# Gated mix of attention and mixer-MLP on one core: layer-norm passes on GpSimd, buffers given back by the last matmul of a group, and a first chunk in four PSUM banks

## The chip, the core and the metric

The kernel runs on one core of a Trainium2 chip. A core has five engines with instruction queues of their own: TensorE (PE in the profile, its weight loads PEld), VectorE (DVE), ScalarE (ACT), GpSimd (POOL) and SyncE (SP, which here only issues transfers). They meet through semaphores. The metric is the device time of one execution in microseconds (us); the time before is 756.24 us, the median of three runs (755.15 to 756.38).

## What is computed

The input x is 2048 x 512 in bf16. Two branches read it and are mixed row by row by a gate:

```python
g = sigmoid((x * gate_w).sum(-1, keepdims=True))
a = softmax(q @ k.T * 16**-0.5) @ v @ wo          # 32 heads of 16, q, k, v = x @ wqkv
h = gelu(layernorm(x) @ w1)                       # 512 x 512
x1 = x + shift(h) @ w2                            # four quarters of h moved by 1, -1, 2, -2 rows
b = x1 + gelu(layernorm(x1) @ w3) @ w4            # 512 x 1792, 1792 x 512
out = g * a + (1 - g) * b
```

## The kernel before

**Work.** The rows are four chunks of 512. A round of attention is one chunk of queries, one group of 8 heads (128 columns of q) and one parity: four heads, one per 32-row strip of TensorE. A round has 64 tiles of scores (16 key tiles by four heads), each 128 keys by 512 queries in one PSUM bank; there are 32 rounds and 2048 tiles. A score matmul is L1313, a PV matmul L1537. The exponential of a tile is taken in one of two ways:

- by ScalarE (L1408), mostly two banks at a time, into `prob`;
- by VectorE (L1439) as an affine map onto the bits of bf16, followed by three shifted copies (L1482 on VectorE, L1484 on GpSimd) of a pair of tiles; all four copies go through PV with weights V or V2, which corrects the map.

The end of a round (`finish_round`, L1548) copies the accumulator (L1558), sends the denominators through DRAM and back, multiplies on GpSimd (L1576) into `oT`, and packs `oT` into `oD` by four transfers (L1580).

**The other work** fills TensorE's time between scores. Projections and MLP matmuls are groups (`gen`, L956; matmuls L964), four column tiles wide, each with one PSUM bank and an evacuation, mostly on VectorE (k L1023, q L1046, V L1063, w1 L1179, w2 L1190, w3 L1211). The gelus run on ScalarE over whole buffers: L1181 once, L1218 four times.

**Layer norms** (`normalise`, L1128): statistics on VectorE (L1122), the reciprocal root on GpSimd (L1131, L1133), then four passes per chunk on VectorE (L1142) from `x_sb` into one of two `xn` buffers, a write to DRAM (L1146), and four transposing loads (L1152) into one of two `xnT` slots, which the groups of w1 or w3 read. There are eight such chunks, four for each norm.

**The start.** 11 matmuls on zeros (L943); 16 transposes of the first chunk's x (L996) into two banks, two quarters each; copies by ScalarE and VectorE (L1006); the q projection, masked into two parities by VectorE (L1038, L1040); the k projection, copied by ScalarE (L1019); then scores.

**The tail.** After the last PV matmul VectorE turns the denominators (L1913 to L1916) and scales (L1926), while TensorE adds in its banks the output projection of head groups LG and above (`known`) and the MLP's result (`add_y`), both at L1890; then the last round's output matmuls (L1932), two evacuations each on VectorE and ScalarE (L1937, L1935), and the output transfers.

**What sets the order.** While the program is built, a planner (`Sim`, `pe_pick`) models the engines with the costs written in the code and picks what each engine issues next; the picks are then emitted as fixed queues. Its parameters (`BASE`, and `STEPS` for every 8 tiles' stage) set priorities. Buffers (`Buf`) are counted: a buffer has `users`, and an op's `frees` are counted off when it is done; at zero the slot goes to the next user. An operation marked `port` on GpSimd is made to wait for the last such operation on VectorE that was emitted before it. In a group, the four column tiles advance separately (`Gen.take`):

```python
o = self.units[k][j]
if min(self.cp) == self.cp[j]:
    for x in self.units[k]:
        if x is not o:
            o.frees += x.frees
            x.frees = []
```

## Time and profile before

| | us |
|---|---|
| median of three runs | 756.24 |
| profiled execution | 755.0 |
| span, first to last instruction | 753.0 |
| PE busy | 738.9 |
| ACT busy | 732.4 |
| DVE busy | 685.8 |
| POOL busy | 458.2 |

The profile is of one execution. A busy PE is modelled from pipelined matmuls and is not PE at its peak. Rows of a timeline give start, duration, engine, line, operation, tiles and count, and in brackets the idle time before and what ended it. Rows of groups give busy us and mean ns of one, then idle time before. In the list of waits the three numbers are us in total, how often, and the longest.

### The profile page before, as it was taken

The numbers are of one execution on the slowest core, as the hardware profiler recorded it, in microseconds if no ns is written. First come the engines' busy times: TensorE is split into PE (matmuls) and PEld (weight loads), VectorE is DVE, ScalarE is ACT, GpSimd is POOL, SyncE is SP. The second block draws the span as 40 slices with busy tenths as digits, with TensorE's granted clock in tenths as the row PEclk, the third lists the DMA queues.
The fourth block names the chain that finished last, engine by engine and source line by source line (L and its number), as shares of the span: only waits on it lengthen the run. The fifth ranks groups of instructions, "written<-read, shape, count | busy, mean of one in ns | idle before, by whom it ended". The sixth has DMA issues, their size and how long they took to land.

```text
span 753.0 us, 23698 instructions
## 1 busy us (share of the span) xinstructions
PE 738.9 (98%) x9520; PEld 213.2 (28%) x9520; DVE 685.8 (91%) x1422; ACT 732.4 (97%) x768; POOL 458.2 (61%) x456
## 2 busy tenths in 40 slices
PE   8999999999999999998999999999999999999997
PEld 4324322223222222222322222222222223222222
DVE  5999999998999999997999999998989999887897
ACT  6999999999999999998999999999999999999995
POOL 2274686657866676665544545557657877774542
PEclk9999999999999999999999999999999999999999
DMA  9403331221123220025001100012000000101001
GB/s 199 143 4 79 68 85 33 66 66 44 57 61 73 69 55 21 21 72 114 8 24 27 38 26 24 10 30 52 21 20 18 20 6 27 28 24 28 20 7 46
DMA packets 67093, 34.59 MB, mean 46 GB/s; under 512 B 46748, under 2 KB 62380, under 8 KB 66984
## 3 DMA queue, kind: packets, MB, share of 16 engines
q1 hardware_dynamic: 66040, 32.56, 17.0%
q8 instruction: 74, 1.21, 0.7%
q10 hardware_dynamic: 944, 0.52, 0.2%
q14 instruction: 35, 0.29, 0.1%
HBM read 17.40 MB, written 6.81 MB: 32 GB/s over the span
## 4 chain that ended last, share of the span: by engine, by line
PE 85%; DVE 5%; ACT 4%; DMA 4%; issue 1%; POOL 0%; SPq 0%; DVEq 0%; POOLq 0%; ACTq 0%
PE banks L1537 30%; PE banks L1313 29%; PE banks L964 24%; ACT prob L1408 3%; DMA pk<-den 2%; DVE prob L1439 2%; DVE prob L1482 1%; DMA den<-accsb 1%; ACT hT L1218 1%; PE banks L943 0%; DVE st L1122 0%; PE banks L1890 0%; DMA zE_dram<-ot 0%; POOL prob L1484 0%; DMA xnT<-xn_dram 0%
## 5 line engine op out<-in xcount | busy, mean ns | idle before, releaser
L1408 ACT ACTIVATE prob<-banks 128x1024 bf16<-128x1024 f32 (+1 forms) x747 | 687.7, 1143 | 6.3 <-PE banks L1313 5.2
L1484 POOL TENSOR_SCALAR prob<-prob 128x1024 uint16<-128x1024 uint16 x394 | 405.7, 1048 | 255.4 <-DVE prob L1482 108.7
L1439 DVE TENSOR_SCALAR prob<-banks 128x512 uint16<-128x512 f32 x551 | 364.0, 683 | 29.6 <-PE banks L1313 25.6
L1537 PE MATMUL banks<-prob,V 128*17 128x512 bf16 (+1 forms) x3707 | 318.3, 382 | 1.3 <-POOL prob L1484 0.6
L1313 PE MATMUL banks<-q,kT 32*128 32x512 bf16 x2048 | 283.2, 385 | 2.8 <-ACT prob L1408 0.9
L1482 DVE TENSOR_SCALAR prob<-prob 128x1024 uint16<-128x1024 uint16 (+1 forms) x437 | 172.6, 440 | 5.8 <-PE banks L1537 1.7
L1313 PEld LDWEIGHTS <-kT 32*128 32x128 bf16 x2048 | 70.9, 91 | 306.5 <-ACT prob L1408 277.2
L1537 PEld LDWEIGHTS <-V 128*17 128x17 bf16 (+1 forms) x3707 | 71.4, 88 | 122.4 <-issue 102.2
L964 PE MATMUL banks<-xnT,w 128*32 128x512 bf16 x1152 | 91.1, 384 | 3.4 <-DMA xnT<-xn_dram 3.4
L964 PE MATMUL banks<-w,hT 128*32 128x512 bf16 x692 | 63.2, 383 | 0.0
L964 PEld LDWEIGHTS <-w 128*32 128x32 bf16 x1920 | 39.7, 95 | 53.3 <-issue 31.4
L1576 POOL TENSOR_TENSOR oT<-accsb,bcs 128x512 bf16<-128x512 f32 x31 | 39.5, 1275 | 21.0 <-DVE prob L1482 8.4
L964 PE MATMUL banks<-w,hB 128*32 128x512 bf16 x448 | 40.0, 382 | 0.0
L964 PE MATMUL banks<-w,w 128*32 128x256 bf16 (+1 forms) x768 | 38.7, 311 | 0.6 <-DVE V L1063 0.4
L975 PE MATMUL banks<-wo,oD 32*128 32x512 bf16 x72 | 27.7, 384 | 0.0
L1211 DVE CAST hT<-banks 128x512 bf16<-128x512 f32 x28 | 19.1, 682 | 5.2 <-PE banks L964 5.2
L1211 DVE CAST hB<-banks 128x512 bf16<-128x512 f32 x28 | 19.0, 682 | 4.6 <-PE banks L964 4.5
L1558 DVE COPY accsb<-banks 128x512 f32<-128x512 f32 x31 | 21.1, 680 | 1.8 <-PE banks L1537 1.7
L964 PE MATMUL banks<-w,wq 128*32 128x512 bf16 x256 | 21.5, 390 | 0.7 <-ACT w L1006 0.7
L964 PEld LDWEIGHTS <-hT 128*32 128x32 bf16 x692 | 15.9, 95 | 20.3 <-issue 13.7
L1122 DVE BATCH_NORM_STATS2 st<-x_sb 128x6 f32<-128x512 bf16 x32 | 21.1, 678 | 0.0
L964 PE MATMUL banks<-wo,oD 128*32 128x512 bf16 x152 | 20.1, 384 | 0.1
(94 smaller groups left out, 259.1 us busy)
## 6 DMA issues: line engine op xcount, KB each, us to landing
bcs<-rr SPq DMA_DIRECT2D x124, 64.0 KB
xn_dram<-xn SPq DMA_DIRECT2D x32, 128.0 KB
w<-in_B_w_dram SPq DMA_DIRECT2D x5, 512.0 KB
oD<-oT SPq DMA_DIRECT2D x124, 16.0 KB
w<-in_B_w_dram SPq DMA_DIRECT2D x4, 448.0 KB
out_dram<-ot SPq DMA_DIRECT2D x14, 128.0 KB
x_sb<-in_A_x_dram SPq DMA_DIRECT2D x3, 512.0 KB
w<-in_A_wqkv_dram SPq DMA_DIRECT2D x2, 256.0 KB
```

Source lines behind the costliest of these rows:

```text
L964: units.append([Op("col", j, lambda j=j, lf=lf, rf=rf, n0=n0, n1=n1, st=st, sp=sp: nc.tensor.matmul(get()[32 * j:32 * j + 32, n0:n1], lhsT ...
L975: o = Op("row", i, lambda: nc.tensor.matmul(get(), lhsT=lf(0, P)[rows], rhs=rf()[rows], start=False, stop=True, tile_position=(32 * i, 0), ...
L1122: a = dve(600, deps, lambda: nc.vector.bn_stats(out=sb.slot[:], in_=x_sb[:, t, :]), prio=6, at=at, acq=[sb])
L1211: pre.append(evac(g, PSUM_NS, lambda ps, m=m: nc.vector.tensor_copy(out=h2()[:, m, :], in_=ps[:])))
L1313: o = Op("row", i, lambda: nc.tensor.matmul(dst(), lhsT=kT[G][32 * i:32 * i + 32, kt * P:(kt + 1) * P], rhs=qbuf[G, c].slot[32 * i:32 * i ...
L1408: job = act(hold, ops, lambda: nc.scalar.activation(out=prob[:, pb.cut(), :].bitcast(BF16), in_=unit()[:, rb.cut(), :], func=ACT.Exp, scal ...
L1439: return nc.vector.tensor_scalar(out=prob[:, b0.cut() if w == 2 else b0.bufs[h0].slot, :], in0=unit()[:, rb.cut() if w == 2 else rb.bufs[0 ...
L1482: return nc.vector.tensor_scalar(out=cut(k), in0=cut(0), scalar1=float(SHIFT * k), scalar2=None, op0=ALU.add)
L1484: return nc.gpsimd.tensor_scalar(out=cut(k), in0=cut(0 if both else 2), scalar1=1.0, scalar2=float(SHIFT * (k if both else 1)), op0=ALU.mu ...
L1537: return nc.tensor.matmul(one(accs[r])[32 * i:32 * i + n, :], lhsT=lhs(n), rhs=rhs(), start=st and not edge, stop=True, tile_position=(0, ...
L1558: e = dve(PSUM_NS, round_ops[r], lambda: nc.vector.tensor_copy(out=ab.slot[:], in_=one(accs[r])), acq=[ab], prio=0, frees=[accs[r], Call(a ...
L1576: n = gp(1250, d3, lambda: nc.gpsimd.tensor_tensor(out=ob.slot[:], in0=ab.slot[:], in1=bb.slot[:], op=ALU.mult), acq=[ob], frees=[ab, bb], ...
```

## The change

It has these parts:

- `normalise` runs its four passes per chunk on GpSimd, with a modelled cost of 592 ns.
- `Gen.take` hands an op's `frees` on to a column tile of the same unit that has yet to issue, instead of gathering them at the last one.
- The first chunk's transposes use four banks, one per quarter. Its k projection is split in two halves of 256 columns (`k_first`), each copied by ScalarE; scores of the first two key tiles need only the first half. The masked q for the first parity is made half by VectorE, half by ScalarE. The second chunk's four copies are all VectorE's, and its transposes wait for the first chunk's.
- The tail: LG is 3, so the groups of head groups 0 to 2 belong to the `wo` groups; `add_y` comes first, and part of the rest is put ahead of the last PV matmuls (`early`).
- Modelled costs: transfers are longer, the first gelu is longer and the later ones shorter.
- The planner's parameters (`STEPS`) are another table; the whole plan is made anew with it. The table is cut below.

```diff
@@ -157,11 +157,10 @@
             return None
         self.cp[j] += 1
         o = self.units[k][j]
-        if min(self.cp) == self.cp[j]:
-            for x in self.units[k]:
-                if x is not o:
-                    o.frees += x.frees
-                    x.frees = []
+        rest = [i for i in range(4) if self.cp[i] < self.cp[j]]
+        if rest:
+            self.units[k][rest[-1]].frees += o.frees
+            o.frees = []
         return o
 
     def row_piece(self, free, know, least):
@@ -479,7 +478,7 @@
     FT = F // P
     assert (S, D, F) == (2048, 512, 1792)
     COL = True
-    LG = 2
+    LG = 3
 
     QAT = 91
     QDUE = 75
@@ -525,211 +524,183 @@
...
@@ -903,7 +874,7 @@
     sim.t_free["SP"] = issue["SP"]
 
     def load_xT(c, k, part, prio):
-        return dma(3100.0, [], lambda: xT_dma(c, part, k)(nc.sync), hold=1280.0, prio=prio,
+        return dma(3500.0, [], lambda: xT_dma(c, part, k)(nc.sync), hold=1280.0, prio=prio,
                    acq=[wb[f"x{c}{part}"]] if k == 0 else [])
 
     def wload(name, src, users):
@@ -990,36 +961,49 @@
     TOT = H * NT * NCH
 
 
-    def x_transposes(c, half, dep):
-        g = gen("t", -1, dep + [j_id], [], due=-9 + half + T1_DUE * c)
-        ks = (half, half + 2)
+    def x_transposes(c, ks, dep):
+        g = gen("t", -1, dep + [j_id], [], due=-9 + ks[0] + T1_DUE * c)
         g.units = [[Op("full", None, lambda k=k, t=t: nc.tensor.transpose(
-            out=one(g.buf).bitcast(BF16)[:, (k // 2) * 512 + t * P:(k // 2) * 512 + (t + 1) * P],
+            out=one(g.buf).bitcast(BF16)[:, ks.index(k) * 512 + t * P:ks.index(k) * 512 + (t + 1) * P],
             in_=x_sb[:, 4 * c + t, k * P:(k + 1) * P], identity=idb[:]), ns=54.0, name="t") for t in range(4)]
             for k in ks]
         g.ops = [o for u in g.units for o in u]
         g.skew = False
-        g.buf.users = 2
-        for k in ks:
-            def cp(k=k):
-                d, s_ = W(f"x{c}0")[:, k, :], one(g.buf).bitcast(BF16)[:, (k // 2) * 512:(k // 2 + 1) * 512]
-                return nc.vector.tensor_copy(out=d, in_=s_) if k % 2 else nc.scalar.copy(out=d, in_=s_)
-            j_xT[c, 0, k] = (dve if k % 2 else act)(340 if k % 2 else 500, g.units[k // 2], cp, prio=0, frees=[g.buf])
+        g.buf.users = len(ks)
+        for n, k in enumerate(ks):
+            on_dve = c or k % 2
+
+            def cp(k=k, n=n, on_dve=on_dve):
+                d, s_ = W(f"x{c}0")[:, k, :], one(g.buf).bitcast(BF16)[:, n * 512:(n + 1) * 512]
+                return nc.vector.tensor_copy(out=d, in_=s_) if on_dve else nc.scalar.copy(out=d, in_=s_)
+            j_xT[c, 0, k] = (dve if on_dve else act)(375 if on_dve else 535, g.units[n], cp, prio=0, frees=[g.buf])
 
 
     j_k = {}
+
+    def k_first():
+        for h in range(2):
+            g = gen("k0", -1, [j_xT[0, 0, 0], j_xT[0, 0, 1], dl_w["k0"]],
+                    [(lambda a, b, k=k: W("k")[:, k, a:b],
+                      lambda k=k, h=h: W("x00")[:, k, 256 * h:256 * h + 256], 0, 256, k == 0, k == KT - 1, 107.5)
+                     for k in range(KT)], due=-3 + h)
+            if h:
+                g.ops[-1].frees += [wb["k"], wb["x00"]]
+            j = act(275, g.units[-1], lambda g=g, h=h: nc.scalar.copy(out=kT[0][:, 256 * h:256 * h + 256],
+                                                                      in_=one(g.buf)[:, 0:256]), prio=0, frees=[g.buf])
+            if h:
+                j_k[0, 0] = j
+            else:
+                j_ka.append(j)
+
+    j_ka = []
 
     def k_proj(G, c, at):
         g = gen(f"k{G}", at, [j_xT[c, 0, k] for k in range(KT)] + [dl_w["k0" if G == 0 else "k"]],
                 [(lambda a, b, k=k: W("k")[:, k, G * P + a:G * P + b],
                   lambda k=k: W(f"x{c}0")[:, k, :]) for k in range(KT)])
         g.ops[-1].frees += [wb["k"], wb[f"x{c}0"]]
-        if G == 0 and c == 0:
-            g.due = -3
-            j_k[G, c] = act(500, g.units[-1], lambda: nc.scalar.copy(out=kT[G][:, 0:512], in_=one(g.buf)[:]), prio=0,
-                            frees=[g.buf])
-            return
-        g.due = 14 * c - 6 if G == 0 else g.due
+        g.due = 14 * c - 11 if G == 0 else g.due
         j_k[G, c] = evac(g, PSUM_NS, lambda ps: nc.vector.tensor_copy(out=kT[G][:, c * 512:(c + 1) * 512], in_=ps[:]),
                          prio=1)
 
@@ -1028,19 +1012,23 @@
 
     def q_proj(G, c, at):
         part = 1 if c else 0
-        g = gen(f"q{G}", at, [j_xT[c, part, k] for k in range(KT)] + [dl_w["q0" if G == 0 else "q"]],
+        g = gen(f"q{G}", at, [j_xT[c, part, k] for k in range(KT if c or G else 2)] + [dl_w["q0" if G == 0 else "q"]],
                 [(lambda a, b, k=k: wq[:, k, G * P + a:G * P + b],
                   lambda k=k: W(f"x{c}{part}")[:, k, :]) for k in range(KT)], due=at + QDUE - QAT if at >= 0 else -4)
         g.ops[-1].frees.append(wb[f"x{c}{part}"])
         qb = qbuf[G, c] = Buf("q", 128)
         if G == 0 and c == 0:
 
-            e1 = dve(680, g.units[-1] + [j_m3], lambda: nc.vector.tensor_scalar(
-                out=qb.slot[:, 0, :], in0=one(g.buf)[:], scalar1=mE[:], scalar2=None, op0=ALU.mult), prio=0, acq=[qb])
-            e2 = dve(680, [e1], lambda: nc.vector.tensor_scalar(
-                out=qb.slot[:, 1, :], in0=one(g.buf)[:], scalar1=mO[:], scalar2=None, op0=ALU.mult), prio=0,
+            e1 = [dve(345, g.units[-1] + [j_m3], lambda: nc.vector.tensor_scalar(
+                out=qb.slot[:, 0, 0:256], in0=one(g.buf)[:, 0:256], scalar1=mE[:], scalar2=None, op0=ALU.mult), prio=0,
+                acq=[qb])]
+            e1.append(act(330, g.units[-1] + [j_m3], lambda: nc.scalar.activation(
+                out=qb.slot[:, 0, 256:512], in_=one(g.buf)[:, 256:512], func=ACT.Copy, scale=mE[:]), prio=0))
+            e1[1].need = qb
+            e2 = dve(680, e1, lambda: nc.vector.tensor_scalar(
+                out=qb.slot[:, 1, :], in0=one(g.buf)[:], scalar1=mO[:], scalar2=None, op0=ALU.mult), prio=0.5,
                 frees=[g.buf])
-            j_q[G, c, 0], j_q[G, c, 1] = e1, e2
+            j_q[G, c, 0], j_q[G, c, 1] = sim.add(Job("POOL", 0.0, 0.0, e1, None, prio=0)), e2
             return
         qf = Buf("qf", 2)
         e = evac(g, PSUM_NS, lambda ps: nc.vector.tensor_copy(out=qf.slot[:], in_=ps[:]), prio=1, acq=[qf])
@@ -1055,7 +1043,7 @@
     def v_proj(u, hh, at):
 
         c = u // 2
-        g = gen("v", at, [j_xT[c, 0, k] for k in range(KT)] + [dl_w[f"v{hh}"]],
+        g = gen("v", at, begun + [j_xT[c, 0, k] for k in range(KT)] + [dl_w[f"v{hh}"]],
                 [(lambda a, b, t=t, k=k: W(f"x{c}0")[:, k, (t % 4) * P + a:(t % 4) * P + b],
                   lambda k=k: W("v")[:, k, 256 * hh:256 * hh + 256], 256 * (t % 2), 256 * (t % 2) + 256, k == 0, k == KT - 1,
                   107.5) for t in (2 * u, 2 * u + 1) for k in range(KT)], due=at + P_V[2])
@@ -1139,17 +1127,17 @@
         last = []
         for t in range(4 * c, 4 * c + 4):
             xb = Buf("xn", 1)
-            g = dve(323, [m], lambda t=t, xb=xb: nc.vector.tensor_scalar(
+            g = gp(592, [m], lambda t=t, xb=xb: nc.gpsimd.tensor_scalar(
                 out=xb.slot[:], in0=x_sb[:, t, :], scalar1=rs[which][:, t:t + 1], scalar2=nm[which][:, t:t + 1],
-                op0=ALU.mult, op1=ALU.add), prio=0.35, acq=[xb], port=True)
+                op0=ALU.mult, op1=ALU.add), prio=0.35, acq=[xb])
             last.append(g)
-            ds.append(dma(2200.0, [g], lambda t=t, xb=xb: nc.sync.dma_start(
+            ds.append(dma(2600.0, [g], lambda t=t, xb=xb: nc.sync.dma_start(
                 out=xn_dram[which, t * P:(t + 1) * P, :], in_=xb.slot[:]), frees=[xb]))
         tb = Buf("xnT", FT if which else KT)
         bx[which, c] = tb
         js = []
         for k in range(KT):
-            js.append(dma(3000.0, ds, hold=1280.0, fn=lambda k=k: nc.sync.dma_start(
+            js.append(dma(3600.0, ds, hold=1280.0, fn=lambda k=k: nc.sync.dma_start(
                 out=tb.slot[:, k, :], in_=xn_dram[which, c * 512:(c + 1) * 512, k * P:(k + 1) * P], transpose=True),
                 acq=[tb] if k == 0 else [], prio=4))
             js[k].need = tb if k else None
@@ -1178,7 +1166,7 @@
                 g.ops[-1].frees += [bx[0, c], wb["1"]]
                 pre.append(evac(g, PSUM_NS, lambda ps, c=c, m=m: nc.vector.tensor_copy(
                     out=hT[:, m, 2 + c * 512:2 + (c + 1) * 512], in_=ps[:])))
-        ge = act(93 + 1700 * KT + 3050, pre, lambda: nc.scalar.activation(
+        ge = act(93 + 1700 * KT + 3450, pre, lambda: nc.scalar.activation(
             out=hT[:, :, 2:2 + S], in_=hT[:, :, 2:2 + S], func=ACT.Gelu_apprx_tanh), prio=0)
         dshift = [1, -1, 2, -2]
         s2 = {}
@@ -1215,7 +1203,7 @@
         ups = [mlp2_up(c, s2, at_of, jgate) for c in cs]
         pre = [j for u in ups for j in u[0]]
         for n, (c, (_, bb, h2, jx1g)) in enumerate(zip(cs, ups)):
-            ge = act(93 + 427 * FT + (0 if n else 3050), pre, lambda h2=h2: nc.scalar.activation(
+            ge = act(93 + 427 * FT + (0 if n else 2750), pre, lambda h2=h2: nc.scalar.activation(
                 out=h2(), in_=h2(), func=ACT.Gelu_apprx_tanh), prio=-1)
             mlp2_down(c, ge, bb, h2, jx1g, at_of)
 
@@ -1305,7 +1293,8 @@
 
     def tile_ok(r, kt):
         c, G, p = rounds[r]
-        return ready_round(r) and j_k.get((G, kt // 4)) is not None and j_k[G, kt // 4].done is not None
+        k = j_ka[0] if G == 0 and kt < 2 else j_k.get((G, kt // 4))
+        return ready_round(r) and k is not None and k.done is not None
 
     def qk_op(r, kt, i, dst, buf, lat):
         c, G, p = rounds[r]
@@ -1391,7 +1380,7 @@
         return NBANK - len(sim.free["bank"]) - act_banks[0] - acc_banks[0]
 
     def room():
-        return sim.free["bank"] and others() < K.LIMD
+        return sim.free["bank"] and others() < (K.LIMD if sim.tiles else NBANK)
 
     def issue_act(got):
         w = len(got)
@@ -1559,7 +1548,7 @@
                 frees=[accs[r], Call(acc_done)])
         d0 = dma(2000.0, [e], lambda: nc.sync.dma_start(out=db.slot[:], in_=ab.slot[0:P:32, :]), prio=1, acq=[db],
                  frees=[ab], hold=580.0)
-        d1 = dma(2000.0, [d0], lambda: nc.sync.dma_start(
+        d1 = dma(2800.0, [d0], lambda: nc.sync.dma_start(
             out=kb.slot[:], in_=db.slot[:].rearrange("j (b e) -> (j b) e", e=16)), prio=1, acq=[kb], frees=[db],
             hold=400.0)
         r1 = dve(160, [d1], lambda: nc.vector.reciprocal(out=kb.slot[:], in_=kb.slot[:]), prio=0)
@@ -1569,7 +1558,7 @@
             out=rb.slot[:].rearrange("j (b e) -> (j b) e", e=16), in_=kb.slot[:]), prio=1, acq=[rb], frees=[kb], hold=400.0)
         d3 = []
         for j in range(4):
-            d3.append(dma(2200.0, [d2], lambda j=j: nc.sync.dma_start(
+            d3.append(dma(3000.0, [d2], lambda j=j: nc.sync.dma_start(
                 out=bb.slot[32 * j:32 * j + 32, :], in_=rb.slot[j, :].partition_broadcast(32)),
                 acq=[] if j else [bb], frees=[rb], prio=1))
             d3[j].need = bb if j else None
@@ -1608,16 +1597,17 @@
         for t in range(4):
             PLAN["w4", 4 * c + t] = int(a + (b - a) * t / 4)
 
-    x_transposes(0, 0, j_x0)
-    x_transposes(0, 1, j_x0)
-    k_proj(0, 0, -1)
+    for k in range(KT):
+        x_transposes(0, (k,), j_x0)
+    k_first()
     q_proj(0, 0, -1)
-    x_transposes(1, 0, j_x1)
-    x_transposes(1, 1, j_x1)
+    begun = [j_ka[0], j_q[0, 0, 0]]
+    x_transposes(1, (0, 2), j_x1 + begun)
+    x_transposes(1, (1, 3), j_x1 + begun)
     for c in range(1, 4):
         k_proj(0, c, 0)
     for u in range(NT // 2):
-        v_proj(u, 0, max(0, P_V[0] * u - P_V[1]))
+        v_proj(u, 0, max(1, P_V[0] * u - P_V[1]))
     for u in range(NT // 2):
         v_proj(u, 1, int(P_V2[0] + (P_V2[1] - P_V2[0]) * u / 8))
     jg = gate(P_G)
@@ -1890,18 +1880,18 @@
             guard(lb[tt], nc.tensor.matmul(bank[tt][32 * j:32 * j + 32, :], lhsT=lf(32 * j, 32 * j + 32), rhs=rf(), start=st,
                                            stop=sp, tile_position=(0, 32 * j), skip_group_check=True))
 
-    def known(tt, gs):
+    def known(tt, gs, st=True):
         for G in gs:
-            into(tt, lambda a, b: oDbuf[c, G].slot[:, tt * P + a:tt * P + b], lambda: wo[:, G, :], G == LG, False)
-
-    def add_y(tt):
-        into(tt, lambda a, b: idf[:, a:b], lambda: y_of(tt), False, False)
+            into(tt, lambda a, b: oDbuf[c, G].slot[:, tt * P + a:tt * P + b], lambda: wo[:, G, :], st and G == LG, False)
+
+    def add_y(tt, st):
+        into(tt, lambda a, b: idf[:, a:b], lambda: y_of(tt), st, False)
 
     c = NCH - 1
 
     tl = max(t for t, _, name, _ in sim.pelog if name == "pv")
     tl = min(t for t, _, name, _ in sim.pelog if name == "pv" and t > tl - 250.0)
-    early = (0, 1) if max(d.done for d in packs) < tl - 500.0 else ()
+    early = (0, 1) if max(d.done for d in packs) < tl + 1500.0 else ()
     for tt in early:
         sim.emit(tl - 1.0, lambda tt=tt: known(tt, range(LG, 4)))
     sim.order.sort(key=lambda x: (x[0], x[1]))
@@ -1914,14 +1904,11 @@
     nc.vector.reciprocal(out=rdl[:], in_=by32(tr[0])[:, :, 0])
     nc.vector.tensor_tensor(out=rdl[:], in0=rdl[:], in1=zL[:], op=ALU.mult)
     nc.vector.transpose(out=by32(tr[1]), in_=rdl[:].unsqueeze(2).to_broadcast([P, NT, 32]))
+    for tt in (1, 3):
+        add_y(tt, tt not in early)
     for tt in range(4):
         if tt not in early:
-            known(tt, range(LG, 3))
-    add_y(1)
-    add_y(3)
-    for tt in range(4):
-        if tt not in early:
-            known(tt, (3,))
+            known(tt, range(LG, 4), tt % 2 == 0)
     for h in range(2):
         nc.vector.tensor_tensor(out=oT[:, h * 256:(h + 1) * 256], in0=acc[:, h * 256:(h + 1) * 256],
                                 in1=tr[1][:, h * 256:(h + 1) * 256], op=ALU.mult)
```

376 lines of the change are left out of this document (174 added, 202 removed).

## The prediction

> **What bounds the kernel now.** I read the page first, then the list of waits, then ScalarE's own timeline.
>
> ```profile
> span 753.0 us, 23698 instructions
> PE 738.9 (98%) x9520; PEld 213.2 (28%) x9520; DVE 685.8 (91%) x1422; ACT 732.4 (97%) x768; POOL 458.2 (61%) x456
> ```
>
> PE and ACT are both full by the page; the waits tell which of them follows the other.
>
> ```profile
> PEld L1313 <- ACT prob L1408: 277.2, 641, 0.6
> ACT prob L1408 <- PE banks L1313: 5.2, 5, 3.4
> ```
>
> The score matmuls (L1313) stand 641 times, 0.43 us each, until an exp has emptied its banks; the exps wait for scores five times, 5.2 us in all. ACT sets the pace, and PE has 0.43 us in hand per round.
>
> ```profile
> 10.29 12.02 ACT L1408 ACTIVATE prob<-banks 128x1024 bf16<-128x1024 f32 x13
> 349.79 2.18 ACT L1408 ACTIVATE prob<-banks 128x1024 bf16<-128x1024 f32 x2 [3.37 <-PE banks L1313]
> 383.02 235.97 ACT L1408 ACTIVATE prob<-banks 128x1024 bf16<-128x1024 f32 x257 [0.28 <-PE banks L1313]
> 633.86 110.05 ACT L1408 ACTIVATE prob<-banks 128x1024 bf16<-128x1024 f32 x119
> ```
>
> So the span is three pieces: 10.29 us to the first exp, then 733.62 us to the end of the last one (633.86 + 110.05 = 743.91), then 9.09 us of tail. In the middle piece ACT loses 6 us, of which 3.37 in one place. A pair of banks takes 235.97 / 257 = 0.918 us of ACT when they follow each other. The change is worth what it does to these three pieces; work that moves between DVE and POOL counts only if it makes one of them late.
>
> **ACT's work: +3.8 us.** The plan is made anew, so I counted the instructions of the built programs. Exps of two banks go from 746 to 751, the one of three banks goes, and one of a single bank comes (1495 tiles become 1503; VectorE's become 545 from 553).
>
> ```profile
> L1408 ACT ACTIVATE prob<-banks 128x1024 bf16<-128x1024 f32 x746 | 686.5, 1142 | 6.3 <-PE banks L1313 5.2 <-POOL prob L1484 0.7
> L1408 ACT ACTIVATE prob<-banks 128x1536 bf16<-128x1536 f32 x1 | 1.5, 1488 | 0.0
> ```
>
> Five pairs are 5 x 0.918 = 4.59. The three banks go with 1.488 less the overlap of neighbours (1.142 - 0.918 = 0.224): 1.26, between 0.92 and 1.49. The single bank is half a pair, 0.46, between 0 and 0.92. Sum 4.59 - 1.26 + 0.46 = +3.8 (3.1 to 4.6). The gelus and their table loads stay.
>
> **VectorE and GpSimd: cost nothing as long as ACT is never late.**
>
> ```profile
> L1484 POOL TENSOR_SCALAR prob<-prob 128x1024 uint16<-128x1024 uint16 x394 | 405.7, 1048 | 255.4 <-DVE prob L1482 108.7 <-PE banks L1537 40.0 <-ACT prob L1408 36.5
> L1439 DVE TENSOR_SCALAR prob<-banks 128x512 uint16<-128x512 f32 x549 | 361.6, 681 | 29.0 <-PE banks L1313 25.1 <-POOL prob L1484 0.3 <-PE banks L1537 0.3
> L1482 DVE TENSOR_SCALAR prob<-prob 128x1024 uint16<-128x1024 uint16 x434 | 172.0, 441 | 5.8 <-PE banks L1537 1.7 <-POOL prob L1484 1.0 <-ACT prob L1408 0.7
> L1142 DVE TENSOR_SCALAR xn<-x_sb,rs,nm 128x512 bf16<-128x512 bf16 x32 | 12.0, 398 | 0.0
> L1131 POOL TENSOR_SCALAR rs<-mv 128x4 f32<-128x4 f32 x8 | 1.6, 195 | 6.6 <-DVE prob L1482 4.7 <-DVE x_sb L1199 1.5
> L1576 POOL TENSOR_TENSOR oT<-accsb,bcs 128x512 bf16<-128x512 f32 x31 | 39.5, 1275 | 21.0 <-DVE prob L1482 8.4 <-DVE xn L1142 3.2 <-DVE mv L1123 2.7
> ```
>
> DVE loses the 32 normalising passes (12.0 us) and 8 first passes (8 x 361.6/549 = 5.3), and gains 46 shifted copies (46 x 172.0/434 = 18.2): about +1 us on 685.8. POOL loses 58 shifted copies (58 x 405.7/394 = 59.7) and gains the 32 passes. None of these shows on POOL before. From 195 ns for 4 elements and 1048 for 1024 the slope is 0.836 ns, so 512 elements take 0.62 us; the ends are 0.195 (L1131) and 1.275 us (L1576, two inputs). I take 0.62, because L1484 is the same operation with one tensor input: 32 x 0.62 = 19.8 us (6 to 41), and POOL ends near 418 us. Both engines stay below ACT, and SP's queue issues the same transfers. The 76 more matmuls on zeros all stand behind a gelu in PE's order, while ACT runs the gelu, and cost nothing there.
>
> The Trainium skill (GPSIMD Engine Reference, section 4.1) speaks against the move: elementwise work on a tile belongs on VectorE. Its section 3.1 has 769 ns for a 512-element loop; by that figure the passes would take an estimated 24.6 us of POOL instead of 19.8, and the sum would stay, since POOL is not the bound.
>
> **The hand-back: -3.4 us.** `take` moves the buffers that a unit gives back to its last issued op, but also when an earlier op has already given them back; then they are counted off twice, and the slot is free one group early. This is the one long stall.
>
> ```profile
> 345.00:350.00 5.00, 1.65 (x22) 0.51 (x19) 1.03 (x2) 1.63 (x3) 2.77 (x3) 1.00 0.43 94
> 345.04 2.43 SPq L1152 DMA_TRANSPOSE xnT<-xn_dram  x2
> 347.67 0.40 PE L964 MATMUL banks<-xnT,w 128*32 128x512 bf16 x4 [2.48 <-DMA xnT<-xn_dram]
> 348.94 0.40 PE L964 MATMUL banks<-xnT,w 128*32 128x512 bf16 x4 [0.88 <-DMA xnT<-xn_dram]
> ```
>
> The first row gives busy us of PE, PEld, DVE, ACT and POOL: ACT works 1.63 of 5 us. The transposing load of the last chunk's xnT stands ahead of the last w3 group of chunk 1, which reads the same slot, so that group waits for a load it never needed (2.48 + 0.88 us), and the scores behind it on PE wait too. In the new order those loads stand behind that group and it waits for no DMA. What is late next there is the gelu behind the last hT evacuation, for which ACT waited nothing before. I take the whole 3.4 (0 to 3.4).
>
> **The start: -1.5 us.**
>
> ```profile
> 4.62 1.35 PE L996 MATMUL banks<-idb,x_sb 128*128 128x128 bf16 x16
> 5.56 1.07 ACT L1006 COPY w<-banks 128x512 bf16<-128x512 bf16 x2 [2.26 <-PE banks L996]
> 6.01 0.76 DVE L1006 COPY w<-banks 128x512 bf16<-128x512 bf16 x2 [3.86 <-PE banks L996]
> 6.69 1.05 PE L964 MATMUL banks<-w,wq 128*32 128x512 bf16 x16 [0.72 <-ACT w L1006]
> 8.65 0.59 ACT L1019 CAST kT<-banks 128x512 bf16<-128x512 f32 x1 [2.02 <-PE banks L964]
> 9.86 0.60 PE L1313 MATMUL banks<-q,kT 32*128 32x512 bf16 x5
> 10.39 1.06 PE L964 MATMUL banks<-w,w 128*32 128x256 bf16 x32
> L1926 DVE TENSOR_TENSOR oT<-banks,accsb 128x256 bf16<-128x256 f32 x2 | 0.8, 419 | 0.0
> ```
>
> Two chunk quarters shared a bank, so each copy waited for 8 transposes. With four banks it waits for 4 (1.35/16 x 4 = 0.34), at 5.2; the q projection starts as the transposes end, 5.97, and ends at 7.05 instead of 7.74. The k projection comes in halves of 256 columns, 0.53 each, the first at 7.6. ACT masks half of q (0.42 as in L1926) and copies the first kT half (some 0.4, between 0.2 and 0.59) by 8.05, scores start at 8.1, the first exp at 8.5: 1.8 us early. In the new order the second chunk's 16 transposes stand between the next scores, and all four of its copies are DVE's, so I give back 0.3: -1.5 (0 to -1.8).
>
> **The tail: -0.75 us.**
>
> ```profile
> 737.73 1.28 POOL L1576 TENSOR_TENSOR oT<-accsb,bcs 128x512 bf16<-128x512 f32 x1
> 739.03 2.97 SPq L1580 DMA_DIRECT2D oD<-oT  x4
> 744.33 1.05 PE L1890 MATMUL banks<-wo,oD 128*32 128x512 bf16 x16
> 745.19 1.90 PE L1890 MATMUL banks<-w,idf 128*32 128x512 f32 x16
> 746.52 0.76 DVE L1926 TENSOR_TENSOR oT<-banks,accsb 128x256 bf16<-128x256 f32 x2
> 746.91 1.05 PE L1890 MATMUL banks<-wo,oD 128*32 128x512 bf16 x16
> 747.77 1.05 PE L1932 MATMUL banks<-woL,oT 128*32 128x512 bf16 x16
> ```
>
> Behind the last PV matmul PE has 48 records before the output matmuls at 747.77, while DVE has the first half of oT at 746.9. Now the first 16 are done earlier (LG=3), 8 of the other 16 stand ahead of the last four PV matmuls, and 1.90 + 0.53 remain: the output matmuls start near 747.0. The 8 early ones wait for oD. Here oD's last transfer is issued by 742.0, and at some 1.3 us more it lands under 6 us after oT's start at 737.73; in the new order 8 exps (7.3 us) lie between what oT waits for and those 8 matmuls, so no wait (bounds +1.5 to -0.75).
>
> **Sum.** 753.0 + 3.8 - 3.4 - 1.5 - 0.75 = 751.15 us of span, 1.85 less. The profiled execution took 755.0 us, 2.0 around its span, and becomes 753.15. The median of the runs, 756.24, becomes **754.4**.
>
> **Rivals.**
> *POOL's queue turns late (slower).* xn has two slots, so each chunk's third pass waits for a write-out.
>
> ```profile
> 38.86 1.78 DMA den<-accsb
> L1482 DVE TENSOR_SCALAR prob<-prob x437: 284/419/1249, 12.7 to 743.7; 128x1024 uint16<-128x1024 uint16 x145, 128x512 uint16<-128x512 uint16 x1
> ```
>
> A small transfer takes 1.78; one pass lies beside it, so POOL stands some 1.2 us per chunk. Each pass also waits, as POOL's other instructions do, for the last DVE instruction on the port that the two share. Shifted copies are queued behind it, PV on PE needs them in order, and scores stand behind PV. It decides from 0.43 us of lateness, PE's margin per round. Four of eight chunks late by 1.2 give +4.8: 759.2. For: 10 of the 32 passes stand within the first 60 exps, and a shifted copy on DVE took up to 1249 ns against a median of 419, so something holds it at times. Against: DVE's queue stood behind the same two slots, POOL idles 255 us before L1484, and chunk 0's transposing loads now stand 34 exps ahead of their first reader (20 before; the other chunks 20 or more), though SP now issues its write-outs and loads ahead of the gate's transfers. The Trainium skill (SBUF — State Buffer, on the shared port pair) has a GpSimd op and a two-port DVE op lock each other out for a whole instruction; the 1249 ns agrees without proving it.
>
> *The stall stays*, because the hand-back is not what made the load early, or another wait takes its place: 754.4 + 3.4 = 757.8. Against: the new order shows no wait there.
>
> *The start gives nothing*, since scores wait for what now stands between them: 755.9. For: DVE's eight copies and masks are in one queue.
>
> *The remaining 2.7 us of ACT's idle time go as well*, since the plan's transfer times are raised: 751.7.
>
> **How the numbers follow.** Forecast 0.40 (own range 753 to 755.7), POOL late 0.18, stall stays 0.10, start gives nothing 0.17, more idle goes 0.15. A measurement of this kernel tells about 0.2%, 1.5 us, from no change: faster is below 754.7, slower above 757.8. Of the forecast 0.30 lies below; with the last rival and a little of the third, faster 0.48. Slower takes POOL late and half of the stall, 0.23; the rest, 0.29, is within. The range 751.5 to 758.2 leaves out most of the first rival and little else.
>
> **What would show it.** First exp near 8.5; no wait of PE on xnT near 345 us and ACT idle there under 1 us; 752 exps in the middle piece at 0.918 per pair; output matmuls under 3 us behind the last PV; xn on POOL at 0.62. It is wrong if waits of ACT for L1302 (the scores' new line) exceed 5 us in all, or if one stands beside a pass on POOL.

## The result and the profile after

The changed kernel takes **752.88 us** (median of 5 runs, 751.38 to 753.84) against 756.3 for the kernel before, run beside it (755.15 to 757.71): ratio 0.9937, 95% interval 0.9911 to 0.9964. The medians differ by 3.4 us. Forecast was 754.4, 1.85 us below before, with a range of 751.5 to 758.2. The profiled execution took 751.38 us with a span of 749.6; the forecast for it was 753.15 and 751.15.

Line numbers have moved: exps are L1397, scores L1302, PV L1526, groups of matmuls L935, the normalising passes L1130, shifted copies L1471 (VectorE) and L1473 (GpSimd). First the page and the list of waits (us in all, times, longest):

```profile
span 749.6 us, 23875 instructions
PE 735.7 (98%) x9588; PEld 213.0 (28%) x9588; DVE 692.9 (92%) x1430; ACT 734.5 (98%) x773; POOL 422.9 (56%) x430
```

```profile
PEld L1302 <- ACT prob L1397: 284.6, 646, 1.5
...
ACT prob L1397 <- PE banks L1302: 1.5, 4, 0.7
...
ACT L1397 <- PE banks L1526: 0.7, 1, 0.7
```

ScalarE still sets the pace: scores stand 646 times until an exp has emptied their banks. Its waits for scores fell from 5.2 us to 1.5, and the longest from 3.4 to 0.7. Its timeline gives the three pieces:

```profile
8.81 19.57 ACT L1397 ACTIVATE prob<-banks 128x1024 bf16<-128x1024 f32 x21 [0.21 <-PE banks L1302]
28.79 44.38 ACT L1397 ACTIVATE prob<-banks 128x1024 bf16<-128x1024 f32 x48 [0.40 <-PE banks L1302]
...
77.12 55.29 ACT L1397 ACTIVATE prob<-banks 128x1024 bf16<-128x1024 f32 x60 [0.19 <-PE banks L1302]
133.11 40.44 ACT L1397 ACTIVATE prob<-banks 128x1024 bf16<-128x1024 f32 x44 [0.70 <-PE banks L1302]
...
183.20 163.45 ACT L1397 ACTIVATE prob<-banks 128x1024 bf16<-128x1024 f32 x178
...
605.38 1.28 ACT L1397 ACT_TABLE_LOAD   x1 [0.74 <-PE banks L1526]
606.67 134.51 ACT L1397 ACTIVATE prob<-banks 128x1024 bf16<-128x1024 f32 x147
```

| piece | before | forecast of its change | after | change |
|---|---|---|---|---|
| to the first exp | 10.29 | -1.5 | 8.81 | -1.48 |
| first to last exp | 733.62 | +3.8 - 3.4 = +0.4 | 741.18 - 8.81 = 732.37 | -1.25 |
| tail | 9.09 | -0.75 | 8.42 | -0.67 |
| span | 753.0 | -1.85 | 749.6 | -3.4 |

The brackets inside the middle piece sum to 0.40 + 0.19 + 0.70 + 0.74 = 2.0 us, where the same rows of before had 5.9 (0.78, 0.50, 0.31, 3.37, 0.67, 0.28). The row at 183.20 runs on without a bracket to 346.65: the idle stretch of 3.37 us is gone. The middle piece is shorter by 3.9 us of idle time and longer by 2.7 us of work, which the groups show (busy us, mean ns):

```profile
L1397 ACT ACTIVATE prob<-banks 128x1024 bf16<-128x1024 f32 x751 | 689.9, 1141 | 2.0 <-PE banks L1302 1.5
L1397 ACT ACTIVATE prob<-banks 128x512 bf16<-128x512 f32 x1 | 0.8, 762 | 0.0
L1471 DVE TENSOR_SCALAR prob<-prob 128x1024 uint16<-128x1024 uint16 x480 | 198.1, 455 | 4.7 <-PE banks L1526 1.9 <-ACT prob L1397 0.3 <-issue 0.2
L1130 POOL TENSOR_SCALAR xn<-x_sb,rs,nm 128x512 bf16<-128x512 bf16 x32 | 24.3, 768 | 6.7 <-DVE nm L1123 3.4 <-issue 1.7 <-DVE prob L1471 0.8
```

689.9 + 0.8 against 686.5 + 1.5 before. A pass on GpSimd takes 768 ns.

### The profile page after: what moved, and what is told of

It reads as the page before. It is cut to its first block, busy times and chain, and to the rows that moved or that the text cites. A ratio compares the mean times of both kernels' runs of the same rounds, so it can differ in the third digit from the quotient of the medians.

```text
span 749.6 us, 23875 instructions
## 1 busy us (share of the span) xinstructions
PE 735.7 (98%) x9588; PEld 213.0 (28%) x9588; DVE 692.9 (92%) x1430; ACT 734.5 (98%) x773; POOL 422.9 (56%) x430
## 4 chain that ended last, share of the span: by engine, by line
PE 77%; ACT 15%; issue 3%; DVE 3%; POOL 1%; DMA 0%; SPq 0%; ACTq 0%; DVEq 0%; POOLq 0%
PE banks L1526 27%; PE banks L1302 26%; PE banks L935 22%; ACT prob L1397 14%; DVE prob L1471 1%; ACT hT L1169 1%; POOL prob L1473 1%; PE banks L1859 1%; DVE prob L1428 1%; PE banks L914 0%; POOL xn L1130 0%; DMA gpk<-zE_dram 0%; ACT L1397 0%; SPq L1099 0%; ACT L1169 0%
## 5 line engine op out<-in xcount | busy, mean ns | idle before, releaser
L1397 ACT ACTIVATE prob<-banks 128x1024 bf16<-128x1024 f32 x752 | 690.4, 1141 | 2.0 <-PE banks L1302 1.5
L1473 POOL TENSOR_SCALAR prob<-prob 128x1024 uint16<-128x1024 uint16 x336 | 346.1, 1044 | 269.7 <-DVE prob L1471 143.9
L1428 DVE TENSOR_SCALAR prob<-banks 128x512 uint16<-128x512 f32 x543 | 359.6, 684 | 29.8 <-PE banks L1302 25.6
L1526 PE MATMUL banks<-prob,V 128*17 128x512 bf16 (+1 forms) x3683 | 319.1, 382 | 1.3 <-POOL prob L1473 1.1
L1302 PE MATMUL banks<-q,kT 32*128 32x512 bf16 x2048 | 282.2, 385 | 6.4 <-ACT prob L1397 3.8
L1471 DVE TENSOR_SCALAR prob<-prob 128x1024 uint16<-128x1024 uint16 (+1 forms) x483 | 198.7, 454 | 4.7 <-PE banks L1526 1.9
L1302 PEld LDWEIGHTS <-kT 32*128 32x128 bf16 x2048 | 70.9, 91 | 312.9 <-ACT prob L1397 284.6
L1526 PEld LDWEIGHTS <-V 128*17 128x17 bf16 (+1 forms) x3683 | 69.7, 88 | 115.4 <-issue 98.9
L935 PE MATMUL banks<-xnT,w 128*32 128x512 bf16 x1152 | 90.9, 383 | 0.2 <-ACT prob L1397 0.2
L935 PE MATMUL banks<-w,hT 128*32 128x512 bf16 x692 | 66.8, 384 | 0.0
L935 PEld LDWEIGHTS <-w 128*32 128x32 bf16 x1936 | 41.0, 95 | 49.6 <-issue 28.1
L935 PE MATMUL banks<-w,w 128*32 128x256 bf16 (+1 forms) x784 | 39.7, 308 | 0.0
L935 PE MATMUL banks<-w,hB 128*32 128x512 bf16 x448 | 38.5, 383 | 0.0
L1130 POOL TENSOR_SCALAR xn<-x_sb,rs,nm 128x512 bf16<-128x512 bf16 x32 | 24.3, 768 | 6.7 <-DVE nm L1123 3.4
L935 PE MATMUL banks<-wo,oD 128*32 128x512 bf16 x168 | 22.8, 384 | 0.1
L935 PEld LDWEIGHTS <-hT 128*32 128x32 bf16 x692 | 15.6, 95 | 19.2 <-issue 15.4
```

What stands on the lines that cost most here:

```text
L935: units.append([Op("col", j, lambda j=j, lf=lf, rf=rf, n0=n0, n1=n1, st=st, sp=sp: nc.tensor.matmul(get()[32 * j:32 * j + 32, n0:n1], lhsT ...
L1130: g = gp(592, [m], lambda t=t, xb=xb: nc.gpsimd.tensor_scalar(out=xb.slot[:], in0=x_sb[:, t, :], scalar1=rs[which][:, t:t + 1], scalar2=nm ...
L1302: o = Op("row", i, lambda: nc.tensor.matmul(dst(), lhsT=kT[G][32 * i:32 * i + 32, kt * P:(kt + 1) * P], rhs=qbuf[G, c].slot[32 * i:32 * i ...
L1397: job = act(hold, ops, lambda: nc.scalar.activation(out=prob[:, pb.cut(), :].bitcast(BF16), in_=unit()[:, rb.cut(), :], func=ACT.Exp, scal ...
L1428: return nc.vector.tensor_scalar(out=prob[:, b0.cut() if w == 2 else b0.bufs[h0].slot, :], in0=unit()[:, rb.cut() if w == 2 else rb.bufs[0 ...
L1471: return nc.vector.tensor_scalar(out=cut(k), in0=cut(0), scalar1=float(SHIFT * k), scalar2=None, op0=ALU.add)
```

## Experiments

The planner makes a new order after almost any edit, and then everything moves at once. So most of these kernels leave the planner's decisions as they are and change only what is emitted at one place; "all else in place" means that. The ratios are to the kernel before, with the 95% interval.

**One thing needs no run.** With the old `take` put back into the changed kernel, the planner writes the same instructions in the same order on every engine. In the changed kernel's plan the new hand-back changes nothing.

### hb_before: the new hand-back alone

```diff
 (before)
-        if min(self.cp) == self.cp[j]:
...
+        rest = [i for i in range(4) if self.cp[i] < self.cp[j]]
+        if rest:
+            self.units[k][rest[-1]].frees += o.frees
+            o.frees = []
```

> The kernel before with the new hand-back alone; its plan stays row for row up to the load of the last chunk's xnT, which now stands behind the w3 group that reads the slot. Theory: the long idle of ScalarE at 349.8 us (3.37) goes, so under 0.7 us remains there. ScalarE's exps become 747 pairs, 3 of three banks and 1 single (746, 1 and 0 before), worth 0.92 + 2 x 1.26 + 0.46 = +3.9 us, so the middle piece changes by +0.5 in all and the time is 756 to 758, no gain by the hand-back alone. Rival (another wait takes its place, or the load was not the cause): over 2 us of idle stay within 345 to 355 us and the time is near 760.

Measured: 765.67 us, ratio 1.0099 (1.0075 to 1.0124), slower than either theory. ScalarE's timeline:

```profile
193.43 154.58 ACT L1407 ACTIVATE prob<-banks 128x1024 bf16<-128x1024 f32 x168 [0.35 <-PE banks L1312]
...
363.51 15.38 ACT L1407 ACTIVATE prob<-banks 128x1024 bf16<-128x1024 f32 x16 [0.64 <-PE banks L1536]
...
450.29 21.25 ACT L1407 ACTIVATE prob<-banks 128x1024 bf16<-128x1024 f32 x23 [5.41 <-PE banks L1536]
472.46 13.05 ACT L1407 ACTIVATE prob<-banks 128x1024 bf16<-128x1024 f32 x14 [0.92 <-PE banks L1536]
486.62 106.73 ACT L1407 ACTIVATE prob<-banks 128x1024 bf16<-128x1024 f32 x116 [1.11 <-PE banks L1536]
```

The exps run from 193.43 to 348.01 with no break, so the hand-back is what put the load too early, and correcting it removes the idle stretch. But from there on the order is another one, made with a table of parameters that was not made for it. It has new waits, 5.41 us at 450 the longest, and ScalarE is busy 737.3 us instead of 732.4 (747 pairs, 3 of three banks and 1 single, as expected). What makes TensorE late at 450 was not followed.

### load_late and load_early: the load by itself

The same load is moved in SyncE's queue, and nothing else: later in the kernel before, earlier in the changed one. Two of the four loads were on the wrong side; these two are moved.

```diff
-                acq=[tb] if k == 0 else [], prio=4))
+                acq=[tb] if k == 0 else [], prio=4, name="moved" if (which, c) == (1, 3) and k < 2 else ""))
...
-        self.emit(self.t, self.in_port_order(e, j.fn) if j.port else self.reads(j))
+        self.emit(self.t + (4500.0 if j.name == "moved" else 0.0), ...)      # -4500.0 in load_early
```

> The kernel before with all instructions of TensorE, VectorE, ScalarE and GpSimd as they were; only the transposing loads of the last chunk's xnT are issued 4.5 us later in SyncE's queue, so that they stand behind the w3 group that reads the slot. Theory (that load alone makes the long idle): the 3.37 us at 349.8 go, the span falls from 753.0 to 749.6, ratio 0.9955. Rival (another wait comes last there, or the load is then late for its own readers): at least half of the 3.4 us stay or come back, ratio 0.998 or more.

> The changed kernel with the same edit the other way: the transposing loads of the last chunk's xnT issued 4.5 us earlier, so that two of them stand ahead of the last w3 group that reads the slot, all else in place. Theory: TensorE waits there for the load and ScalarE idles 2.5 to 4 us near 345; the span is 752 to 753.5 and the time 2.5 to 4 us over the changed kernel on the same chip. Rival (the changed plan has slack there): idle under 1 us and no change.

> The changed kernel as it is, as the base of the other three on one chip: ratio to before 0.991 to 0.997, first exp at 8.8, ScalarE idle 2.0 us between first and last exp.

> The kernel before with the loads of the last chunk's xnT 4.5 us later, once more, as the base of the next two on one chip: ratio to before 0.989 to 0.994, first exp at 10.3 to 10.5, no idle of ScalarE over 1 us between first and last exp.

| kernel | us, median (range) | ratio to before |
|---|---|---|
| changed_again | 752.33 (751.53 to 752.9) | 0.9928 (0.9904 to 0.9953) |
| load_late | 750.95 (750.67 to 753.2) | 0.9917 (0.9892 to 0.9943) |
| late_base, load_late's kernel once more | 750.69 (749.64 to 751.42) | 0.992 (0.9904 to 0.9936) |
| load_early | 756.63 (754.14 to 759.28) | 0.9994 (0.9975 to 1.0013) |

Moving two loads in the kernel before gives all that the whole change gives; moving them the other way in the changed kernel takes all of it back: load_early is 4.3 us above changed_again, where 2.5 to 4 was expected. In it TensorE waits again for the load, and ScalarE for TensorE:

```profile
345.99 0.38 PE L935 MATMUL banks<-xnT,w 128*32 128x512 bf16 x1 [2.08 <-DMA xnT<-xn_dram]
346.74 1.02 ACT L1397 ACTIVATE prob<-banks 128x1024 bf16<-128x1024 f32 x1 [2.03 <-PE banks L1302]
348.50 0.59 PE L935 MATMUL banks<-xnT,w 128*32 128x512 bf16 x1 [1.05 <-DMA xnT<-xn_dram]
349.75 1.02 ACT L1397 ACTIVATE prob<-banks 128x1024 bf16<-128x1024 f32 x1 [1.98 <-PE banks L1302]
```

In load_late the last exps before the gelus end on time, at 349.44:

```profile
339.25 10.19 ACT L1408 ACTIVATE prob<-banks 128x1024 bf16<-128x1024 f32 x11 [0.76 <-PE banks L1313]
```

Its span is 748.8 us, 4.2 under before, where 3.4 was expected; by the medians it is 0.8%, some 6 us. So the idle stretch costs more than its own length; the next run looks for the rest.

### filled_wait: the same wait, with TensorE kept busy

```diff
 (before; o is the first matmul of the waiting group's k = 0, then of k = 1; n = 14, then 5)
...
+        def issue():
+            for _ in range(n):
+                for i in range(4):
+                    nc.tensor.matmul(one(accs[r])[32 * i:32 * i + DH + 1, 0:384], lhsT=zero[:, 0:DH + 1], rhs=zero[:],
+                                     start=False, stop=True, tile_position=(0, 32 * i), skip_group_check=True)
+            return fn()
...
```

> The kernel before with the long wait left in, but 14 x 4 matmuls on zeros ahead of the first waiting matmul and 5 x 4 ahead of the second, so that TensorE is busy while it waits for the load. Theory (the idle stretch itself lowers the granted clock behind it, and that costs about 1 us over the 3.4 of idle): the clock in 350 to 354 us is 1.00 instead of 0.58, the mean clock 0.999 or more instead of 0.991 to 0.998, ScalarE still idles some 3.4 us at 350, the time is 1 to 2 us below before, ratio 0.997 to 0.9985. Rival (the clock falls for another reason, or its fall costs nothing): clock near 0.6 to 0.8 behind the wait, or ratio 0.999 to 1.002.

Measured: 754.16 us (752.7 to 755.34), ratio 0.996 (0.9945 to 0.9976). The wait is still there:

```profile
344.80 2.44 SPq L1152 DMA_TRANSPOSE xnT<-xn_dram  x2
345.08 2.46 PE L1892 MATMUL banks<-zero 128*17 128x384 bf16 x56
347.51 0.40 PE L964 MATMUL banks<-xnT,w 128*32 128x512 bf16 x4
347.73 1.00 PE L1892 MATMUL banks<-zero 128*17 128x384 bf16 x20
...
349.54 1.94 ACT L1411 ACTIVATE prob<-banks 128x1024 bf16<-128x1024 f32 x2 [3.16 <-PE banks L1316]
```

ScalarE loses 3.16 us there, against 3.37 before. What differs is the granted clock. Busy time by stretches (PE, PEld, DVE, ACT, POOL with counts, then TensorE's clock), of before and of filled_wait:

```profile
350.00:354.00 4.00, 4.00 (x36) 0.80 (x36) 3.64 (x7) 3.84 (x4) 1.05 (x1) 0.58 0.36 89
```

```profile
345.00:350.00 5.00, 5.00 (x101) 2.52 (x98) 0.99 (x2) 1.84 (x3) 2.72 (x3) 1.00 0.46 96
350.00:354.00 4.00, 4.00 (x57) 1.25 (x58) 3.98 (x8) 3.97 (x4) 1.89 (x2) 1.00 0.39 84
```

After the idle wait TensorE has a clock of 0.58 and issues 36 matmuls in 4 us; after the filled one it has 1.00 and issues 57. The same eight PV matmuls behind the wait, of before and of filled_wait:

```profile
350.79 1.03 PE L1537 MATMUL banks<-prob,V 128*17 128x512 bf16 x8
```

```profile
350.22 0.61 PE L1540 MATMUL banks<-prob,V 128*17 128x512 bf16 x8
```

The kernel before is granted 0.989 to 0.998 as a mean over a run (63 runs beside these experiments), filled_wait 0.999 to 1.0. Among the 63, time goes with the clock: the 14 runs at 0.997 or 0.998 have a mean of 755.8 us, the 32 from 0.994 to 0.996 757.2, the 17 below that 759.8. So of some 6 us that the early load costs, about half (1 - 0.996 = 0.4%, 3 us) is the lowered clock and half the wait itself. The theory held; its price was 1 to 2 us, the measured one 3, with an interval of 1.8 to 4.2.

The profile of before is a mild case. Its mean clock is 0.998, which the 4 us at 0.58 account for (1.7 us of 753), and its span is only 1.5 us over that of filled_wait. No trace of before shows where its slower runs, at 0.99, lose the rest.

### xn_vector and late_xn: the normalising passes on the other engine

```diff
 (xn_vector, in the changed kernel; late_xn the other way round in load_late's kernel)
-            g = gp(592, [m], lambda t=t, xb=xb: nc.gpsimd.tensor_scalar(
+            g = gp(592, [m], lambda t=t, xb=xb: nc.vector.tensor_scalar(
...
-        self.emit(self.t, self.in_port_order(e, j.fn) if j.port else self.reads(j))
+        self.emit(self.t, self.in_port_order("DVE" if j.name == "xn" else e, j.fn) if j.port else self.reads(j))
```

The second pair of lines gives the passes the `port` rule of their new engine: in late_xn they wait for the last such operation on VectorE, and in xn_vector the next such operation on GpSimd waits for them.

> The changed kernel with every instruction at its place, except that the 32 normalising passes are issued on VectorE where GpSimd had them. Theory (moves between the two engines cost nothing while ScalarE is never late): GpSimd loses 24.3 us, VectorE gains about 12.5, time within 1 us of the changed kernel, 752 to 754. Rival (VectorE at 692.9 of 749.6 has no room, so each 0.4 us pass makes a shifted copy or a first pass late): 32 x 0.4 = up to +12.8, so 757 to 765, with new idle of ScalarE for scores.

> The base with the 32 normalising passes issued on GpSimd at the places where VectorE had them, all else in place. Theory (both engines have room, nothing that ScalarE needs waits): within 1 us of the base. If the 2 to 3 us that the passes cost on VectorE in the changed order are VectorE's lack of room, the base gets 1 to 2.5 us faster. Rival of the prediction (GpSimd's queue turns late, here without a plan that knows of the passes): 3 to 5 us slower than the base, with ScalarE waiting for scores beside the passes.

xn_vector: 755.36 us, ratio 0.9965 (0.9945 to 0.9985), against 0.9937 and 0.9928 for the changed kernel; its span is 752.5, 2.9 over it. The intervals overlap, but all 12 runs (754.07 to 758.07) lie above all 11 of the changed kernel (751.38 to 753.84), which ran on another chip or in another session. ScalarE's waits for scores are twice as long:

```profile
ACT prob L1397 <- PE banks L1302: 3.2, 8, 0.8
```

late_xn: 756.58 us (754.6 to 759.31) against 750.69 for its base on the same chip; ratios 0.9993 (0.9977 to 1.001) and 0.992 (0.9904 to 0.9936). Its waits:

```profile
POOL xn L1142 <- DVE prob L1482: 6.5, 5, 1.9
...
DVE x_sb L1199 <- POOL xn L1142: 4.5, 6, 1.6
...
ACT prob L1408 <- PE banks L1313: 3.5, 7, 0.8
```

So the move is not free by itself in either direction. Put on an engine whose order was not made for them, the passes cost some 2.5 us (0.9965 against 0.9928 to 0.9937) and 6 us: on GpSimd they stand until VectorE's shifted copies are done (6.5 us), and VectorE's later update of `x_sb` then stands behind them (4.5 us). The first of these waits is one that the program makes by its `port` rule; no run leaves the rule out. That is the prediction's first rival, and larger than it was priced (4.8). It did not come in the changed kernel: there the passes stand only 0.8 us for shifted copies, and no engine is listed as waiting for them.

### price_768: the planner told the true duration

```diff
-            g = gp(592, [m], lambda t=t, xb=xb: nc.gpsimd.tensor_scalar(
+            g = gp(768, [m], lambda t=t, xb=xb: nc.gpsimd.tensor_scalar(
```

> The changed kernel with one figure of its planner changed: a normalising pass on GpSimd is planned at 768 ns, as the trace has it, instead of 592. The plan is made anew: 763 exps of two banks instead of 751 and a single one, and 522 first passes on VectorE instead of 545. Theory (ScalarE's work sets the span): (763 - 751) x 0.9186 - 0.76 = +10.3 us, 762 to 764. Rival (the plan was late because the passes were priced too low, so the true price takes idle time away): at most the 2 us of ScalarE's idle time go, so by this 751 to 753 if the extra exps are covered.

Measured: 778.38 us, ratio 1.0266 (1.0236 to 1.0296). The extra exps are there:

```profile
L1397 ACT ACTIVATE prob<-banks 128x1024 bf16<-128x1024 f32 x763 | 701.9, 1146 | 15.6 <-DVE x_sb L1178 5.9 <-PE banks L1302 5.3 <-PE banks L1526 4.1
```

701.9 against 690.7 is +11.2 us, near the 10.3 expected; but ScalarE also idles 15.6 us before exps instead of 2.0. The theory had the work right and left out that a new order without a table made for it has new waits. hb_before showed the same. In both, a plan made anew under a table that was made for another plan gave a slower kernel; a table made for the new cost was not tried.

### two_banks, late_banks and whole_mask: the start

```diff
 (two_banks, changed kernel: quarters 2 and 3 go to the second halves of the banks of 0 and 1)
+        gb = g.buf if c else pair.setdefault(ks[0] % 2, g.buf)
...
 (late_banks, load_late's kernel: quarters 2 and 3 get banks of their own)
+        tb = lambda k: banks_of((k,))[:, k] if c == 0 and k > 1 else one(g.buf)
...
 (whole_mask, changed kernel; ScalarE's half is left out)
-                out=qb.slot[:, 0, 0:256], in0=one(g.buf)[:, 0:256], scalar1=mE[:], ...
+                out=qb.slot[:, 0, :], in0=one(g.buf)[:], scalar1=mE[:], ...
```

> The changed kernel with every instruction at its place, except that chunk 0's four quarters share two banks again, as before. Theory: each copy waits for 8 transposes instead of 4, both copies of ScalarE start near 5.6 instead of 5.22, the q projection near 6.6 instead of 5.85, so the first exp is 0.6 to 0.75 us later, 9.4 to 9.55, and the span grows by as much. Rival (the start is bound by the masks and the order of ScalarE's queue): first exp at 8.8 to 9.0 and no change.

> The base with chunk 0's quarters transposed into four banks instead of two, all else in place. Theory of the start (each copy waits for 4 transposes, not 8): copies at 5.2 instead of 5.6 to 5.7, q projection at 5.9 instead of 6.7 to 6.8, first exp 0.6 to 0.8 us earlier, 9.6 to 9.8. If ScalarE alone sets the pace, the span falls by as much; rival (what is gained at the start comes back as idle time, as in whole_mask): the first exp is earlier and the span the same within 0.3 us.

> The changed kernel with every instruction at its place, except that VectorE makes the first mask of q whole (512 columns) and ScalarE makes none of it. Theory (the halves run one behind the other, 0.49 + 0.47 us and a hand-over, and ScalarE's copies of kT wait behind its half): VectorE is done at some 7.8, both kT copies are earlier, first exp at 8.3 to 8.45 instead of 8.81, span 0.35 to 0.5 less. Rival (kT's halves come last anyway): first exp at 8.7 to 8.9.

two_banks: 753.94 us, ratio 0.995 (0.9933 to 0.9968); first exp at 9.88, 1.07 later, more than expected, since here the transposes also wait for a copy to leave the shared bank, which they did not in the kernel before:

```profile
5.82 0.38 PE L970 MATMUL banks<-idb,x_sb 128*128 128x128 bf16 x4 [0.67 <-ACT w L982]
...
6.98 1.05 PE L935 MATMUL banks<-w,wq 128*32 128x512 bf16 x16
```

Its span is 752.2, 2.6 over the changed kernel: the late start not only reached the end, it grew on the way, with ScalarE waiting 2.1 us for TensorE between 77 us and the first gelu instead of 0.9, and 0.58 us behind the next gelus, at 363, instead of nothing. The reason was not followed.

late_banks: 750.94 us against 750.69 for its base, and the first exp at 10.02 against 9.97. The expectation failed: the q projection did not start earlier than in the base (6.31).

```profile
5.29 1.07 ACT L1007 COPY w<-banks 128x512 bf16<-128x512 bf16 x2 [1.98 <-PE banks L997]
...
6.41 1.05 PE L964 MATMUL banks<-w,wq 128*32 128x512 bf16 x16 [0.27 <-ACT w L1007]
```

ScalarE's two copies end at 5.29 + 1.07 = 6.36, and only then the projection starts. In the changed kernel it starts at 5.85, as ScalarE's first copy ends, because there it is put into the queue behind two quarters (`range(KT if c or G else 2)`). So the four banks alone show no gain in the old queue. A few tenths could hide in the scatter of the start: with two banks the first exp came at 9.97 (late_base), 10.29 (before) and 10.44 us (load_late). In the new queue they are needed, at least against two_banks.

whole_mask: 752.06 us (751.25 to 752.47), ratio 0.9925 (0.9898 to 0.9951), not told apart from changed_again. The mask and what follows:

```profile
6.75 0.75 DVE L1022 TENSOR_SCALAR q<-banks,mE 128x512 bf16<-128x512 f32 x1 [0.76 <-PE banks L935]
...
7.98 19.58 ACT L1396 ACTIVATE prob<-banks 128x1024 bf16<-128x1024 f32 x21
...
360.60 1.28 ACT L1396 ACT_TABLE_LOAD   x1 [0.81 <-PE banks L1525]
```

```profile
360.57 1.28 ACT L1397 ACT_TABLE_LOAD   x1 [0.33 <-PE banks L1526]
```

The first exp comes 0.80 us earlier than in changed_again (8.78), more than expected, of which some 0.3 is an earlier start of the first copies (4.90 against 5.18). The last row is changed_again's: both kernels load the table of exp at 360.6 us, and both spans are 749.8. The 0.8 came back as idle time of ScalarE, which waited for TensorE (98% busy): 2.0 us between 94 and 361 us instead of 0.9. Here a gain at the start did not reach the end, while the loss in two_banks did. What exactly holds TensorE there stays open.

## Why the prediction was right, and where it was wrong

- **What bounds the kernel.** Right: exps pace the middle piece, and its change is the change of ScalarE's work and of its idle time.
- **ScalarE's work, +3.8.** Too high: +2.7. The pairs gave 689.9 - 686.5 = +3.4 and not 4.59, since the mean pair fell from 0.9202 to 0.9186 us; the rest is 0.8 - 1.5. Over 746 pairs a change of 0.0016 us is 1.2 us, more than the forecast resolved.
- **VectorE and GpSimd cost nothing.** Right for this plan, with the sizes off: a pass takes 0.768 us and not 0.62, GpSimd is busy 422.9 us (forecast 418), and VectorE gained 7.1 us instead of 1, since its shifted copies went from 172.0 to 198.1 us, +26.1 where 18.2 was summed. The Trainium skill (GPSIMD Engine Reference, section 3.1) has 769 ns for a 512-element loop; the trace agrees. The step was wrong as a statement about the move: xn_vector and late_xn show that it costs 2.5 to 6 us where the order is not made for it.
- **The hand-back, -3.4.** The right place, and the largest term, but it was mis-sized and its cause was only half right. Moving the load is worth 4.2 us in the profiled span and some 6 us in the medians, above the bound of 3.4 that the prediction gave, because the wait also lowers the clock behind it; the prediction read the stretch of the wait, 345 to 350 us, and not the one behind it with its clock of 0.58. And in the changed kernel it isn't the new `take` that keeps the load behind the group: the plan is the same without it. In the kernel before it is (hb_before). Which part of the new plan, its table or its costs, keeps the load late was not taken apart.
- **The start, -1.5.** It measured -1.48 to the first exp, by another sum, and that close a match is luck: the start scatters. The first exp came at 8.78 to 9.60 us in five profiles with the changed start and at 9.86 to 10.44 in six with the old one; their means differ by 1.1. The projection started at 5.85, where 5.97 was forecast (its end at 7.05 is a slip: 5.97 + 1.05 is 7.02), but ScalarE's half of the mask waited for VectorE's instead of running beside it, so the first exp came at 8.81 and not at 8.5, and the 0.3 held back for the second chunk was not needed:

```profile
7.07 0.49 DVE L1022 TENSOR_SCALAR q<-banks,mE 128x256 bf16<-128x256 f32 x1 [0.76 <-PE banks L935]
7.59 0.47 ACT L1025 ACTIVATE q<-banks,mE 128x256 bf16<-128x256 f32 x1 [1.30 <-DVE q L1022]
...
8.38 0.39 PE L1302 MATMUL banks<-q,kT 32*128 32x512 bf16 x4 [0.55 <-ACT kT L992]
```

- **The tail, -0.75.** It measured -0.67. TensorE is no longer last: the output matmuls wait for VectorE's scaling.

```profile
743.87 0.76 DVE L1913 TENSOR_TENSOR oT<-banks,accsb 128x256 bf16<-128x256 f32 x2
744.35 1.05 PE L1919 MATMUL banks<-woL,oT 128*32 128x512 bf16 x16 [0.44 <-DVE oT L1913]
```

  The parts of the tail were not tried one by one.
- **The fourth rival** (more idle goes) came in part: besides the long stretch, ScalarE's idle time fell from 2.5 to 2.0 us.
- **The sum.** 1.55 us too long in the span: 1.1 from ScalarE's work, 0.5 from idle time. Against before the gain is 3.4 us by the medians (2.7 to 6.7 by the ratio's interval), about twice the forecast 1.85; the one term that was missing altogether is the clock behind the wait. The terms with the right sign did not add up to a reason, though. The changed kernel and load_late differ by start (8.78 against 10.44), tail (8.47 against 9.03) and middle piece (732.55 against 729.33), and the first two are spent in the third, which has five more pairs. All that the change gains over before, one moved load gains without the rest: 750.95 and 750.69 us. This is also the quickest kernel of the study; it is not told apart from the changed one (0.9917 and 0.992 against 0.9937 and 0.9928).
